# Linear-attention sums on one core: four heads and both signs of phi as one weight, 65 columns instead of 129, two PSUM banks instead of three, with due times and places annealed anew

## The chip, the cores and the metric

The program runs on one core of a Trainium2 chip. The metric is the time of one execution on the device in microseconds. Every time given here is the median of several executions, and the mean granted TensorE clock was between 0.996 and 1.0 in all profiled runs quoted.

Engines are named as in the profile: PE is TensorE, PEld its weight loads, DVE is VectorE, ACT is ScalarE, POOL is GpSimd, SP is SyncE, which issues most of the DMA.

## The reference

Two identical layers, each an attention without softmax over tokens (part A) and a gated MLP (part B), over 2048 tokens of width 512. Only part A is touched. H is 32 heads of width 16.

```python
def _A_ref(x, wqkv, w_phi, wo):                      # x is layer-normed
    q, k, v = ...                                    # [B, H, S, 16] each, from x @ wqkv
    pq = jnp.einsum("bhsd,hdf->bhsf", q, w_phi)
    pk = jnp.einsum("bhsd,hdf->bhsf", k, w_phi)
    phi_q = concatenate([softmax(pq), softmax(-pq)]) # 32 features: both signs of phi
    phi_k = concatenate([softmax(pk), softmax(-pk)])
    kv = jnp.einsum("bhsf,bhsd->bhfd", phi_k, v)     # the sums over all tokens
    z  = jnp.einsum("bhsf->bhf", phi_k)              # and the sum of phi itself
    num = jnp.einsum("bhqf,bhfd->bhqd", phi_q, kv)
    den = jnp.einsum("bhqf,bhf->bhq", phi_q, z)[..., None] + 1e-6
    return (num / den) ... @ wo
# x = x + A(norm(x)); x = x + MLP(norm(x)); twice
```

What matters: `kv` and `z` must be complete over all 16 token tiles (of 128 tokens) before any attention of that layer can start.

## The kernel before

The program is a list of operations, each with an engine, an estimated cost, a due time and the buffers that it takes and uses. When the program is built, a planner puts them in order: at each step it takes, of the operations that could start first, the one with the lowest due time. The order on each engine is then fixed; on the chip, engines only wait for each other's results and for buffers. The due times and a string of places (ACT or DVE for a copy, POOL or DVE for a phi) come from annealing on the planner's own costs.

```python
P, D, H, DH, NB, T, HB = 128, 512, 32, 16, 4, 16, 8
GV = P + 1                                           # 128 columns of v and one column of ones
p_q, p_b = psum("q", 3), psum("b", 5)                # 8 PSUM banks in all
p_ek, p_phi = pool("ek", 4, [2, D]), pool("phiK", 4, [2, D])
p_v = pool("vext", 5, [NB, GV])
# ... cut

class Keys:
    def __init__(self, l, before):
        self.bufs = [Buf(p_q) for _ in range(3)]     # held from the first token tile to R's build
    def tile(self, t, ...):
        # K = x Wk (PE), ek = exp(+-K) (ACT), V = x Wv (PE), vext <- V (ACT or DVE)
        # sk = sums of ek per head and sign (DVE, 128x64 <- 128x1024), 1/sk by ln and exp (ACT)
        # phiK = ek * 1/sk, two halves, each on DVE or POOL
        def kvz():
            for g in range(2 * NB):
                b, s = g // 2, g % 2                 # b: 8 heads, s: sign
                nc.tensor.matmul(self.bufs[g // 3].t[:, (g % 3) * GV:(g % 3 + 1) * GV],
                                 lhsT=ph.t[:, s, b * P:(b + 1) * P], rhs=vx.t[:, b, :],
                                 start=(self.n == 0 and g % 3 == 0), stop=(self.n == T - 1),
                                 skip_group_check=True)
    def build(self, due):                            # R: the sums, masked to each head's own block
        for k in range(3):
            ng = 3 if k < 2 else 2
            # num: R[:, 3k:3k+ng, 0:DH, :] = sums * Mf      128 x (ng*128)
            # den: R[:, 3k:3k+ng, DH, :]   = (z + eps/2) * Mf
# attend(): per token tile three groups of matmuls of R with Eq into PSUM buffers of p_q,
# copied out as N (numerators) and DS (denominators) by ACT or DVE
```

One weight holds eight heads of one sign; its product with `v` of those eight heads is 128x128, of which the mask keeps the eight 16x16 blocks on the diagonal.

The softmax here doesn't subtract the row's maximum and nothing guards it: scores larger than these inputs give would overflow.

Of the kernel before, what the change touches and what calls it, by code (L numbers as in the profile page):

```python
# [8 lines left out]
P = 128  # L9
D = 512  # L10
H = 32
DH = 16
# [7 lines left out]
GV = P + 1  # L20
# [183 lines left out]
DVE0 = (85, 170)  # L204
STATS = (592, 692)
# [11 lines left out]
class K:  # L217
# [9 lines left out]
    "0000010000001001000100000001010000000000101100111000110100010000100001001000000000100100101011010000"  # L227
    "1000000000111101000110100111010010111011010100100110101011010000101011001110000110000000111000000101"
    "1100101010101000101000110000000100000100110010110011011101000010011110010100010111101011111011011010"
# [9 lines left out]
    7238437, 6462738, 6444986, 6386567, 5992333, 6335033, 6406961, 6303369, 5712831, 6413612, 6092682, 6414331,  # L239
    7434675, 6620170, 4674366, 7071562, 5773774, 7071571, 7071548, 7071565, 5376048, 6430379, 5994524, 5038937,  # L240
    5154841, 6509440, 6825368, 6847621, 6377520, 5995707, 6404704, 6443663, 6844264, 5995988, 6959386, 6784947,
    6825065, 6420713, 6382495, 5410283, 6400005, 6216969, 7068818, 6425562, 6371338, 6325356, 5116853, 6509939,
    6325403, 6399345, 6420906, 6420903, 6403761, 5854885, 5527927, 6112383, 6040357, 6246638, 6429204, 6120059,
    6425464, 5996011, 5410344, 5937857, 5997209, 6629949, 6159020, 5837281, 6159017, 5812166, 6376057, 6112054,
    5527770, 5778741, 5859984, 6246016, 5780700, 6191478, 5995462, 6415371, 6420993, 5937862, 6218721, 6366108,
    6398876, 6355933, 6040362, 6353076, 6692318, 6246832, 6301941, 6333817, 6305472, 6420324, 6246635, 6282608,
    6010072, 6010132, 5937718, 5517502, 5527720, 5962872, 6417645, 6375834, 6115594, 6417622, 6376951, 6040201,
    6418805, 6367897, 6418065, 6246853, 6246635, 6280551, 6416172, 6413450, 5812833, 5734989, 5527730, 6415701,
    6589688, 6660152, 6259055, 6293340, 6418857, 6193613, 6400771, 6242577, 5594853, 5897821, 6418101, 6246214,
    6414310, 6418410, 6417781, 6293326, 6418213, 6337803, 6493628, 5823924, 6281803, 6385607, 6385616, 6414319,  # L250
    6392870, 6399165, 6376822, 6423098, 6382355, 6246148, 6189671, 6413294, 5970487, 6354744, 6354741, 6148511,
    6557117, 6415725, 7222162, 6412246, 6420372, 6418246, 6414304, 6330448, 6400107, 6407313, 6121354, 6246632,
    6247421, 6281496, 6418264, 6416104, 6292977, 6417603, 6446115, 6428567, 5823973, 6417942, 6323224, 6435617,
    6413175, 6372016, 6395620, 6424638, 6323105, 6245911, 6245802, 6350052, 6399800, 6339292, 6104846, 6199296,
    6400901, 6500288, 6429150, 6504253, 6415373, 5944333, 5942659, 6414885, 6419661, 6437686, 6424884, 6421739,
    6390896, 7006151, 6419612, 6444868, 6419927, 6419499, 6248090, 6668478, 6424284, 4761373, 6406555, 6435614,
    6323108, 6413172, 6425996, 6391320, 6135302, 6402710, 6374285, 6246461, 6335990, 6412253, 5985101, 5911850,
    6386514, 6397260, 6453191, 6347268, 6424767, 6407286, 6143060, 6143057, 6407535, 6396443, 6128422, 6067112,
    6334982, 7007584, 6247418, 6262299, 6338418, 6339077, 5945577, 5945498, 6399500, 6358459, 6363359, 6335893,
    6334988, 6334985, 6399098, 6149279, 9046332, 6270119, 6128455, 6017799, 5751499, 5578303, 6241820, 6237909,  # L260
    6228313, 6409033, 6434152, 6430501, 4770010, 6328230, 6191571, 6416107, 6349922, 7005684, 6415913, 6160440,
    6270116, 6017016, 6424993, 6190885, 6436945, 6398264, 6385936, 6409019, 6398261, 6830494, 6320125, 6349843,
    6270116, 6301355, 6394746, 6838656, 6782627, 6275299, 6301053, 6290656, 6025116, 5578252, 6382357, 6396063,
    6432980, 6476817, 6211202, 6228770, 6039495, 6004981, 6301064, 6161212, 6348404, 6160934, 6138010, 6350845,
    6275296, 5796164, 6025266, 6407917, 6382458, 6396463, 6502608, 6067109, 6415534, 4853830, 6415237, 5973986,
    6161241, 6353578, 6191119, 6350842, 6702118, 6992600, 6838653, 6366565, 6702501, 6264078, 6413974, 6362908,
    6362904, 6413355, 4467245, 6428734, 6412410, 6795872, 6752777, 6749932, 5860936, 5410347, 6354370, 6416428,
    6376372, 6441207, 6382099, 6417945, 6095059, 5543843, 5639763, 5236921, 6702312, 6802433, 6193610, 6293063,
    6418233, 6412932, 6417391, 6417541, 6412910, 5973743, 6432169, 6353603, 6418389, 6417785, 6418212, 6432986,
    6404484, 6419790, 6403799, 6504104, 6413197, 6402581, 6430185, 6421941, 6427775, 6317437, 6405598, 6149276,  # L270
    6067109, 6421649, 6426875, 6424701, 6424305, 6424600, 6431997, 6419066, 6427616, 6151465, 6421964, 6428658,
    6427976, 6422709, 6152793, 6428425, 6417633, 6429195, 6318384, 6422133, 6429703, 6429560, 6364528, 6798754,
    5236191, 6414580, 6296106, 6296113, 6054709, 5898871, 6296074, 5892919, 5617487, 5397065, 5397082, 3706746,
    5397079, 6419465, 5126265, 5416638, 3706278, 6415767, 6422610, 5124110, 6416965, 6625553, 5123800, 6416602,
    6419816, 6420908, 5396532, 5396822, 5497114, 7088606, 5592093, 5592116, 8111730, 6424461, 6419795, 6461520,
    6418906, 6421398, 6625766, 6420136, 6413037, 6424609, 6419798, 6425587, 5125608, 4328837, 3879494, 5115836,
    5126573, 6460663, 5847129, 6363148, 6422584, 5092781, 6419709, 5924498, 6237696, 6420096, 6427244, 6401061,
    6420862, 6421285, 6206071, 6156101, 6156036, 5302232, 5547741, 6373591, 6421404, 6060028, 6419415, 6048257,
    6419829, 5124239, 5126428, 6420346, 6431104, 6414424, 6420420, 6301789, 6982400, 5678438, 6154618, 6458766,
    6154597, 6156591, 6458649, 6427548, 6633825, 6444562, 6420766, 6006011, 6507274, 6421320, 6253412, 5547942,  # L280
    6421596, 6431444, 6336831, 6017869, 6957435, 6881846, 6972027, 6421334, 6350314, 6426586, 6250179, 6349612,
    6420979, 6409085, 6420596, 6419900, 6431585, 6431582, 6421968, 6430875, 6335448, 6348116, 6156140, 6448961,
    6426886, 6426258, 6434836, 6426677, 6425021, 6423370, 6420949, 5962145, 6205350, 6420178, 6420997, 6507473,
    6421435, 6337297, 5302335, 6253340, 6409377, 6446621, 6483667, 6272602, 6426074, 6429263, 6350262, 6426486,
    6421195, 6426208, 6448726, 6422715, 6336723, 6422336, 6423095, 6426531, 6349600, 6426322, 6453653, 6424950,
    6449358, 6416002, 6423415, 6411076, 6419851, 6422066, 6423162, 6425195, 6425012, 6424458, 6425647, 6425793,
    6423997, 6422141, 6425481, 6428769, 6424841, 6423823, 6423627, 6429536, 6425171, 6427675, 6426450, 6428704,
    6421366, 6431460, 6430235, 6423699, 6427448, 6423529, 6424778, 6431481, 6423189, 6279797, 6279298, 6418638,
    6421996, 6516407, 6517705, 6519047, 6426870, 6424741, 6423138, 6423148, 6422363, 6422859, 6424168, 6417327,
    6425272, 6425495, 6425628, 6424234, 6422881, 6424086, 6426119, 6424179, 6422682, 6424910, 6418638, 6426823,  # L290
    6425100, 6433715, 6430613, 6425871, 6428635, 6428822, 6424500, 6428773, 6427578, 6426097, 6424080, 6425359,
    6428061, 6424746, 6430015, 6420709, 6395980, 6491720, 6421893, 6336657, 6337082, 6422630, 6426207, 6426179,
    6424375, 6421663, 6425660, 6425930, 6422794, 6422276, 6425132, 6335341, 6425761, 6404996, 6383616, 6385581,
    6426169, 6427999, 6425677, 6426328, 6428760, 6428757, 6424969, 6428920, 6424083, 6424141, 6428548, 6424537,
    6428822, 6428197, 6427995, 6421391, 6428775, 6432602, 6425470, 6426425, 6424396, 6426336, 6426162, 6425753,
    6426483, 6430576, 6428349, 6429772, 6429237, 6429182, 6430031, 6402283, 6432374, 6426676, 6430764, 6435892,
    2595536, 5127000, 3705691, 6419739, 6236173, 3879702, 5846911, 6434442, 6421288, 6156356, 6312974, 6424365,
# [674 lines left out]
```

## Time and profile before

| | before |
|---|---|
| median time | 390.2 us (389.81 to 390.4, three executions) |
| span of the profiled execution | 388.6 us |
| PE busy, DVE busy | 379.0 us, 309.5 us |
| sums: matmuls, columns, start to start | 256, 129, 57 ns |
| last sum of layer one, first MLP matmul | 55.06 us, 67.38 us |
| first attention matmul of layer two | 243.29 us |

These are lines of the profile's page for the kernel before: the span, the busy time of PE with its share and count, and the chain of work that ended last, by engine.

```profile
span 388.6 us, 7611 instructions
PE 379.0 (98%) x2789; PEld 231.2 (60%) x2833; DVE 309.5 (80%) x785; ACT 217.7 (56%) x569; POOL 43.5 (11%) x45
PE 82%; DVE 7%; ACT 4%; DMA 3%; SPq 2%; issue 2%; DVEq 0%; ACTq 0%
```

PE is named for 82% of the chain. The 98% say less: the end of a matmul in this profile is modelled, and neighbours overlap. The Trainium skill ("Perfetto Trace Analysis", section Identifying the Most-Contended Engine) says that the busy share of matmuls is no good measure of the distance to the limit. So I used starts. In this trace a 512-column matmul is followed after 216 ns, one of 256 columns after 109, of 128 after 56, of 144 after 62. Where a start comes later than that, PE waited. In tables below, *PE waiting* is the sum over neighbouring matmuls of the start-to-start time minus columns/2.4 + 2.5 ns, with gaps left out that are longer by just one matmul's pace (those are records that the trace lacks). At the very start this reading fails: up to 4.7 us in this trace, starts come at half the pace (427 ns at 512 columns, 107 at 128), so waiting is counted from 13 us on. How the start goes differs from run to run: the first `sk` reduction on DVE starts at 11.9 to 12.6 us in the twelve traces of the new order. A time read from a single trace carries some tenths of a us for that reason.

Busy times by stretch, for the kernel before. The columns are the stretch, its length, and busy us (with the count of instructions) of PE, PEld, DVE, ACT and POOL, then PE's clock and the DMA.

```profile
13.00:57.00 44.00, 43.33 (x296) 23.86 (x300) 41.24 (x72) 40.75 (x120) 20.76 (x20) 1.00 0.73 169
57.00:80.00 23.00, 21.43 (x263) 16.59 (x262) 20.90 (x66) 18.52 (x55) 0.00 (x0) 1.00 0.11 22
180.00:250.00 70.00, 69.58 (x494) 43.56 (x500) 49.86 (x90) 48.81 (x121) 13.39 (x12) 1.00 0.09 18
```

From 13 to 57 us layer one's keys and sums are made, and DVE and ACT are nearly as full as PE. From 57 to 80 us attention starts. From 180 to 250 us layer two's sums are finished beside layer one's MLP, and DVE has 20 us free.

A burst of the sums in the timeline of the kernel before (start, length, engine, line, operation; x8 is eight instructions):

```profile
40.61 0.62 PE L678 MATMUL q<-vext,phiK 128*128 128x129 bf16 x8
...
41.07 0.38 PE L647 MATMUL b<-wv,xnTA 128*128 128x512 bf16 x1
```

Eight sums start at 40.61 and the next group starts at 41.07, 0.46 us later: 57 ns each. All 256 take 256 x 57 ns = 14.6 us of PE.

R's build in layer one of the kernel before, on DVE:

```profile
55.20 0.27 DVE L702 SCALAR_TENSOR_TENSOR R<-q,Mf 128x24 bf16<-128x24 f32 x2 [1.13 <-PE q L678]
55.39 1.34 DVE L695 TENSOR_TENSOR R<-q,Mf 128x384 bf16<-128x384 f32 x3
56.65 0.16 DVE L702 SCALAR_TENSOR_TENSOR R<-q,Mf 128x16 bf16<-128x16 f32 x1
```

It runs from 55.20 to 56.81 us, 1.6 us, and no attention can start before it ends.

### The profile page before, as it was taken

What the parts mean: (1) busy time and instruction counts of PE and PEld (TensorE: products, weight loads), DVE (VectorE), ACT (ScalarE), POOL (GpSimd) and SP (SyncE); (2) the same over time, 40 slices, a digit from 0 to 9 for tenths busy, and PEclk for the clock granted to TensorE, in tenths of its full rate; (3) what the DMA queues carried; (4) which work ended last, traced back from release to release, by engine and by line L of the source; (5) the groups of instructions that cost most, each with busy time, mean ns of one, the idle gap of its engine ahead of it and who ended that gap; (6) DMA issues with size and microseconds to landing.
All of it is one profiled execution on the core that took longest, in us unless ns stands there. A gap on an engine that the chain in (4) does not pass through costs nothing.

```text
span 388.6 us, 7611 instructions
## 1 busy us (share of the span) xinstructions
PE 379.0 (98%) x2789; PEld 231.2 (60%) x2833; DVE 309.5 (80%) x785; ACT 217.7 (56%) x569; POOL 43.5 (11%) x45
## 2 busy tenths in 40 slices
PE   8999998999999999999999999999999999999996
PEld 4555565957654554454667655578765545547674
DVE  6999979989999985479767486799997999455243
ACT  6999979744556545134665668976525520443111
POOL 0344620000200400012220122000000000000000
PEclk9999999999999999999999999999999999999999
DMA  8389730122322221102200000022233122201110
GB/s 245 105 187 189 209 102 1 37 55 50 79 57 42 56 53 29 27 16 54 43 0 15 14 15 0 2 33 62 57 71 81 38 51 65 54 7 29 56 35 29
DMA packets 60870, 22.84 MB, mean 59 GB/s; under 512 B 52672, under 2 KB 59808, under 8 KB 60832
## 3 DMA queue, kind: packets, MB, share of 16 engines
q1 hardware_dynamic: 60416, 21.95, 25.6%
q8 instruction: 22, 0.36, 0.4%
q10 hardware_dynamic: 416, 0.39, 0.3%
q14 instruction: 16, 0.13, 0.1%
HBM read 7.91 MB, written 2.10 MB: 26 GB/s over the span
## 4 chain that ended last, share of the span: by engine, by line
PE 82%; DVE 7%; ACT 4%; DMA 3%; SPq 2%; issue 2%; DVEq 0%; ACTq 0%
PE b L829 32%; PE b L862 19%; PE b L765 7%; PE b L641 5%; PE b L647 5%; PE b L715 4%; PE q L678 3%; PE b L805 3%; PE q L733 3%; ACT Eq L719 2%; DMA xnTA<-xn 1%; SPq L486 1%; DMA oT<-o 1%; ACT ek L644 1%; DVE N L564 1%
## 5 line engine op out<-in xcount | busy, mean ns | idle before, releaser
L829 PE MATMUL b<-xnTB,wgu 128*128 128x128 bf16 (+2 forms) x1192 | 149.9, 279 | 0.5
L829 PEld LDWEIGHTS <-wgu 128*128 128x128 bf16 x1200 | 97.8, 98 | 42.7
L862 PE MATMUL b<-wd,hT 128*128 128x512 bf16 (+2 forms) x348 | 82.1, 372 | 0.8
L833 ACT ACTIVATE gu<-b 128x512 bf16<-128x512 f32 (+1 forms) x83 | 48.1, 582 | 48.1 <-PE b L829 45.0
L661 POOL TENSOR_TENSOR phiK<-ek,sk 128x512 bf16<-128x512 bf16 x39 | 42.8, 1114 | 193.4 <-ACT sk L657 145.3
L862 PEld LDWEIGHTS <-hT 128*128 128x128 bf16 (+1 forms) x363 | 34.8, 98 | 34.9 <-DVE hT L837 0.3
L837 DVE TENSOR_TENSOR hT<-gu 128x512 bf16<-128x512 bf16 (+1 forms) x83 | 33.7, 407 | 18.6 <-ACT gu L563 17.0
L644 ACT ACTIVATE ek<-b 128x512 bf16<-128x512 f32 x64 | 36.0, 600 | 16.7 <-PE b L641 16.5
L652 DVE TENSOR_REDUCE sk<-ek 128x64 f32<-128x1024 bf16 x32 | 38.6, 1209 | 8.1 <-ACT ek L644 8.0
L563 ACT CAST gu<-b 128x512 bf16<-128x512 f32 (+1 forms) x46 | 26.1, 566 | 31.7 <-PE b L829 31.4
L719 ACT ACTIVATE Eq<-b 128x512 bf16<-128x512 f32 x64 | 35.4, 623 | 4.7 <-PE b L715 4.5
L564 DVE CAST gu<-b 128x512 bf16<-128x512 f32 (+1 forms) x37 | 25.0, 677 | 13.2 <-PE b L829 13.0
L869 DVE SCALAR_TENSOR_TENSOR X<-b,rsB,X 128x512 bf16<-128x512 f32 (+1 forms) x33 | 23.4, 725 | 15.1 <-PE b L862 15.0
L641 PE MATMUL b<-Wk,xnTA 128*128 128x512 bf16 x125 | 32.5, 379 | 0.4 <-DMA xnTA<-xn 0.3
L765 PE MATMUL b<-wo,oT 128*128 128x512 bf16 x121 | 31.7, 379 | 1.2 <-DMA oT<-o 0.8
L563 ACT CAST N<-q 128x384 bf16<-128x384 f32 (+1 forms) x63 | 27.9, 461 | 8.4 <-DVE pr L758 3.2
L647 PE MATMUL b<-wv,xnTA 128*128 128x512 bf16 x121 | 31.7, 379 | 0.4
L715 PE MATMUL b<-xnTA,Wq 128*128 128x512 bf16 x125 | 30.7, 379 | 0.2
L733 PE MATMUL q<-R,Eq 128*128 128x144 bf16 x256 | 26.8, 226 | 1.1 <-ACT N L563 0.5
L733 PEld LDWEIGHTS <-Eq 128*128 128x128 bf16 x256 | 19.9, 98 | 11.3 <-issue 1.4
L769 DVE TENSOR_TENSOR X<-X,b 128x512 bf16<-128x512 bf16 x32 | 21.5, 676 | 2.3 <-PE b L765 2.2
L610 DVE BATCH_NORM_STATS2 bstA<-X 128x6 f32<-128x512 bf16 x32 | 21.2, 681 | 1.8 <-DMA X<-in_A_x_dram 1.6
(71 smaller groups left out, 396.6 us busy)
## 6 DMA issues: line engine op xcount, KB each, us to landing
out_dram<-X SPq DMA_DIRECT2D x15, 128.0 KB, 1.7
X<-in_A_x_dram SPq DMA_DIRECT2D x6, 256.0 KB, 3.4
wgu<-in_B_W_gate_dram SPq DMA_DIRECT2D x4, 344.0 KB, 3.8
wgu<-in_B_W_up_dram SPq DMA_DIRECT2D x4, 344.0 KB, 4.6
wd<-in_B_W_down_dram SPq DMA_DIRECT2D x5, 256.0 KB, 4.5
wv<-in_A_wqkv_dram SPq DMA_DIRECT2D x2, 256.0 KB, 4.2
wo<-in_A_wo_dram SPq DMA_DIRECT2D x4, 128.0 KB, 3.1
oT<-o SPq DMA_TRANSPOSE x28, 2.4
```

Source lines behind the costliest of these rows:

```text
L563: both = {"ACT": ("ACT", act(cols), lambda: nc.scalar.copy(out=out_(), in_=in_()), False), "DVE": ("DVE", dve(cols), lambda: nc.vector.ten ...
L641: k = op("PE", mm(4, 512), due, lambda: [nc.tensor.matmul(kp.t[:], lhsT=xnTA[c][:, b, cols], rhs=Wk2[:, b, :], start=(b == 0), stop=(b == ...
L644: e = [op("ACT", act(512), due, lambda s=s: nc.scalar.activation(out=ek.t[:, s, :], in_=kp.t[:], func=AF.Exp, scale=1.0 - 2.0 * s), [k], [ ...
L647: v = op("PE", mm(4, 512), due_v, lambda: [nc.tensor.matmul(vp.t[:], lhsT=xnTA[c][:, b, cols], rhs=wv[:, b, :], start=(b == 0), stop=(b == ...
L661: e.tensor_tensor(out=ph.t[:].rearrange("p s (h f) -> p (s h) f", f=DH)[:, lo:lo + n], in0=ek.t[:].rearrange("p s (h f) -> p (s h) f", f=D ...
L715: q = op("PE", mm(4, 512), due(c, b), lambda b=b, qp=qp: [nc.tensor.matmul(qp.t[:], lhsT=Wq2[:, m, b * P:(b + 1) * P], rhs=xnTA[c][:, m, : ...
L719: done.append(op("ACT", act(512), due(c, b), lambda b=b, s=s, qp=qp: nc.scalar.activation(out=Eq[c][:, b, s, :], in_=qp.t[:], func=AF.Exp, ...
L733: pe.append(op("PE", mm(len(groups), GE), due, lambda ps=ps, groups=groups: [nc.tensor.matmul(ps.t[:, n * GE:(n + 1) * GE], lhsT=Eq[c][:, ...
L765: a = op("PE", mm(4, 512), due + 3, lambda: [nc.tensor.matmul(yp.t[:], lhsT=oT.t[:, b, :], rhs=wo[:, b, :], start=(b == 0), stop=(b == NB ...
L829: nc.tensor.matmul(ps.t[:, q * W:(q + 1) * W], lhsT=wgu[:, s, b, g * P:(g + 1) * P], rhs=xT.t[:, b, 0:W], start=(b == 0), stop=(b == NB - 1))
L833: nc.scalar.activation(out=gu.t[:, 0, 0:cols], in_=gp.t[:, 0:cols], func=AF.Relu)
L862: nc.tensor.matmul(yp.t[:, 0:c1 - c0], lhsT=h.t[:m, f * W + i * P:f * W + (i + 1) * P], rhs=wd[:m, f, c0:c1], start=(f == 0), stop=(f == N ...
```

## The change

One weight now holds four heads with both signs (4 x 2 x 16 = 128 columns), so its moving operand is only those four heads' 64 columns of v and the ones: 65 columns instead of 129. There are still eight matmuls and eight weight loads per token tile. The eight results fit two banks (4 x 65 = 260 columns each), so that `q` gives one bank to `b`. The layout of ek and phi follows. R's build takes four quarters of 64 partitions, since a sign is now half of the partitions, and R must be zeroed once. DUE and PLACE are new throughout.

```diff
+NG = 2 * NB
+HG = HB // 2
+GQ = P // 2
-GV = P + 1
+GV = GQ + 1
+SUMS = (8 * 40, 8 * 40 + 170)
-    p_q, p_b = psum("q", 3), psum("b", 5)
+    p_q, p_b = psum("q", 2), psum("b", 6)
-    p_ek, p_phi = pool("ek", 4, [2, D]), pool("phiK", 4, [2, D])
+    p_ek, p_phi = pool("ek", 4, [NG, 2, GQ]), pool("phiK", 4, [NG, 2, GQ])
-    p_v = pool("vext", 5, [NB, GV])
+    p_v = pool("vext", 5, [NG, GV + 1])
+    c_r0 = op("DVE", dve(1152, 4), 15000, lambda: nc.vector.memset(R[:], 0.0), ...)
-            self.bufs = [Buf(p_q) for _ in range(3)]
+            self.bufs = [Buf(p_q) for _ in range(2)]
-                for g in range(2 * NB):
-                    b, s = g // 2, g % 2
-                    nc.tensor.matmul(self.bufs[g // 3].t[:, (g % 3) * GV:(g % 3 + 1) * GV],
-                                     lhsT=ph.t[:, s, b * P:(b + 1) * P], rhs=vx.t[:, b, :],
+                for g in range(NG):
+                    b, k = g // 2, g % 2
+                    nc.tensor.matmul(self.bufs[k].t[:, b * GV:(b + 1) * GV],
+                                     lhsT=ph.t[:, g, :, :].rearrange("p s e -> p (s e)"), rhs=vx.t[:, g, 0:GV],
-            for k in range(3):                     # three num of up to 128x384, three den
+            for k in range(2):
+                for s in range(2):                 # four num of 64x256, four den
+                    rows, to = slice(s * GQ, (s + 1) * GQ), slice(k * GQ, (k + 1) * GQ)
+                    ...
# cut: the same access patterns in ek, sk, phi and vext; all of DUE (2112 numbers before, 2117 after)
# and most of PLACE (301 characters)
```

## The prediction

> **What bounds the kernel now.** TensorE, nearly everywhere. The page gives PE 379.0 of 388.6 us busy, but its ends are modelled, so I read starts. In the trace 512-column matmuls follow each other every 216 ns, 256 columns every 109, 128 every 56, 144 every 62: the rate at which columns stream ("TensorE: Matmul & The Clock Gate" of the Trainium skill, section on the back-to-back gap, has N/2.4 + 2.5 ns; the trace agrees). Against that rate, leaving out doubled gaps that are missing records, the stream loses only about 8 us: 1.3 before the first matmul, some 2.5 more to 10 us, 3.3 between 60 and 80 us, 3.4 after the last matmul. The granted clock is 1.0. DVE and ACT come near their limit only early: windows of 10 us from 10 to 50 us have DVE 9.0 to 10.0 and ACT 9.3 to 10.0 busy; 50 to 60 has slack. From 180 to 250 us, where layer two's sums are made, DVE has 50 of 70 us.
>
> **What the change removes.** The sums phi-transposed times v: 8 matmuls of 129 columns per token tile, 256 in all. In the timeline a burst of 8 starts at 40.61 and the next group at 41.07 us: 57 ns each, 14.5 us in all (the chain gives this line 3.1%). Now the moving part is 65 columns; weight loads stay at 256 of 128x128. The streaming rate would give 30 ns, but each matmul needs its own weight load: in the trace the next load starts 2 ns after a matmul's start, and where the engine had been waiting, the matmul followed its load by 31 ns (transposes at 10.73 us). So 33 ns at least; I estimate 36, range 30 to 45. Saving: 256 x (57 - 36) = 5.3 us (range 3 to 7).
>
> **What it adds.** A memset of R (about 0.4 us DVE, early). Building R: four products of 64 partitions x 256 and four small ones, instead of three of up to 128x384 (548 ns) and three small. Before it took 55.20 to 56.81 us; my estimate after is 2.1, so +0.5 us per layer, mostly covered by queries' matmuls.
>
> **What it moves.** Attention's three products per tile now share two PSUM banks. The timeline at 62 to 66 us shows PE already waiting for copies N and DS (0.42 and 0.49 us); this may grow by tenths. The rest gets six banks, which helps early. Due times and places are annealed again: I give that +-1.5 us.
>
> **How much counts.** Layer two's half of the sums lies in a dense matmul stream with slack on DVE and ACT: its 2.6 us should come through in full. Layer one's lies where DVE and ACT are also full, so part turns into waiting before 80 us: I count 1.4 us. Sum about 4 us: 390.2 to 386.2 us. Range 382.8 to 389.4. Faster by over 2% (under 382.4): 0.08; within 2%: 0.91; slower: 0.01.
>
> **What would show it.** Sums' matmuls starting every 30 to 45 ns instead of 57; PE busy down by some 5 us; layer two's attention starting (first matmul with R after 240 us) 3 us earlier or more; more PE waiting on ACT or DVE before 80 us, not after; R's build about 2 us.
>
> **What would make it wrong.** If the pair of load and matmul can't go below 50 ns, the gain is 1.5 us. If two banks make attention's matmuls wait at 57 to 80 and 240 to 255 us, the gain is lost. If six banks and the new order also remove the waiting between 60 and 80 us, the gain is 7 or 8 us.

## The result, and the profile after

The kernel after takes 388.21 us (387.5 to 388.71, six executions) beside 390.49 us (six executions) of the kernel before. The ratio is 0.9942, 95% interval 0.9928 to 0.9957: a gain of 0.58%, or 2.3 us. A ratio here is the mean time of one kernel's fast runs over that of the other's fast runs of the same rounds, so it is not quite the ratio of the medians.

| | before | after |
|---|---|---|
| median time beside each other | 390.49 us | 388.21 us |
| span of the profiled execution | 388.6 us | 386.3 us |
| PE busy, DVE busy | 379.0, 309.5 us | 374.1, 315.3 us |
| sums: start to start (median) | 57 ns | 32 ns |
| PE waiting 13 to 57 us | 0.9 us | 3.4 us |
| PE waiting 57 to 80 us | 3.0 us | 3.7 us |
| last sum of layer one, first MLP matmul | 55.06, 67.38 us | 55.33, 68.28 us |
| first attention matmul of layer two | 243.29 us | 240.37 us |

The same lines of the page, kernel after:

```profile
span 386.3 us, 7626 instructions
PE 374.1 (97%) x2787; PEld 225.2 (58%) x2831; DVE 315.3 (82%) x799; ACT 212.0 (55%) x559; POOL 45.3 (12%) x46
PE 76%; DVE 9%; ACT 3%; issue 2%; DMA 2%; POOL 0%; DVEq 0%; ACTq 0%
```

PE has 4.9 us less to do by this count, yet the time fell by only 2.3. Its share of the chain fell and DVE's rose. The stretches of the kernel after:

```profile
13.00:57.00 44.00, 41.62 (x297) 20.82 (x302) 43.20 (x72) 41.27 (x123) 20.75 (x19) 1.00 0.69 169
57.00:80.00 23.00, 20.86 (x222) 14.72 (x222) 22.05 (x77) 16.61 (x49) 0.00 (x0) 1.00 0.13 22
180.00:250.00 70.00, 68.96 (x520) 42.50 (x527) 52.50 (x104) 48.37 (x126) 15.54 (x13) 1.00 0.07 14
```

In the first stretch DVE's busy time rose from 41.24 to 43.20 of 44 us although it ran the same number of instructions there, 72, and PE's fell. The last sum of layer one started 0.3 us *later* than before, in spite of shorter sums (0.3 us is about what the start of a trace varies by; that it is not earlier is what counts). At the first attention matmul of layer two the kernel is 2.9 us ahead: all of the gain was made between 68 and 240 us, and 0.7 us of it was lost again after that.

A burst of the sums in the timeline of the kernel after, and the next group:

```profile
52.95 0.42 PE L719 MATMUL q<-vext,phiK 128*128 128x65 bf16 x8
...
53.20 0.59 PE L760 MATMUL b<-xnTA,Wq 128*128 128x512 bf16 x2
```

Eight sums in 0.25 us, 31 ns each. The shortening itself came as large as it could: 256 x (57 - 32) ns = 6.4 us of PE, more than the 5.3 predicted. R's build in layer one, kernel after:

```profile
55.56 0.43 DVE L741 TENSOR_TENSOR R<-q,Mf 64x256 bf16<-64x256 f32 x1 [0.40 <-PE q L719]
...
57.78 0.16 DVE L747 SCALAR_TENSOR_TENSOR R<-q,Mf 64x16 bf16<-64x16 f32 x1
```

It runs from 55.56 to 57.94 us, 2.4 us, 0.8 longer than before (predicted 0.5).

Layer one's half of the saving is 3.2 us, and yet the first MLP matmul comes 0.9 us later: about 4 us went somewhere before 68 us. Three candidates: DVE sets the pace there so that PE's saving is worth nothing (my theory, in part from the prediction); the longer build of R; two banks for attention. A fourth came from the trace and is shown with its experiments: the new order lets DVE run into POOL.

### The profile page after: what moved, and what is told of

It is laid out like the page before. It is cut to its first block, busy times and chain, and to the rows that moved or that the text cites. A ratio compares the mean times of both kernels' runs of the same rounds, so it can differ in the third digit from the quotient of the medians.

```text
span 386.3 us, 7626 instructions
## 1 busy us (share of the span) xinstructions
PE 374.1 (97%) x2787; PEld 225.2 (58%) x2831; DVE 315.3 (82%) x799; ACT 212.0 (55%) x559; POOL 45.3 (12%) x46
## 4 chain that ended last, share of the span: by engine, by line
PE 76%; DVE 9%; ACT 3%; issue 2%; DMA 2%; POOL 0%; DVEq 0%; ACTq 0%
PE b L874 34%; PE b L907 19%; PE b L810 6%; PE b L682 4%; PE b L688 4%; PE q L778 3%; PE b L850 2%; ACT Eq L764 2%; PE b L760 2%; DVE sk L693 2%; PE q L719 1%; DVE phiK L702 1%; DMA oT<-o 1%; DVE bstA L651 1%; DMA xnTA<-xn 1%
## 5 line engine op out<-in xcount | busy, mean ns | idle before, releaser
L702 POOL TENSOR_TENSOR phiK<-ek,sk 128x512 bf16<-128x512 bf16 x40 | 44.6, 1133 | 191.3 <-ACT sk L698 106.1
L605 DVE CAST gu<-b 128x512 bf16<-128x512 f32 (+1 forms) x42 | 28.0, 669 | 15.7 <-PE b L874 15.7
L604 ACT CAST gu<-b 128x512 bf16<-128x512 f32 (+1 forms) x41 | 23.2, 565 | 22.8 <-PE b L874 21.8
L778 PE MATMUL q<-R,Eq 128*128 128x144 bf16 x256 | 27.8, 226 | 1.4 <-ACT DS L604 0.8
L604 ACT CAST N<-q 128x384 bf16<-128x384 f32 (+1 forms) x60 | 26.7, 466 | 4.1 <-DVE pr L803 2.9
L855 ACT ACTIVATE gr<-b 128x192 bf16<-128x192 f32 (+1 forms) x19 | 5.8, 308 | 31.8 <-PE b L850 31.8
```

The costliest lines, as they stand in the source:

```text
L604: both = {"ACT": ("ACT", act(cols), lambda: nc.scalar.copy(out=out_(), in_=in_()), False), "DVE": ("DVE", dve(cols), lambda: nc.vector.ten ...
L702: e.tensor_tensor(out=ph.t[:].rearrange("p g s (h f) -> p (g s h) f", f=DH)[:, lo:lo + n], in0=ek.t[:].rearrange("p g s (h f) -> p (g s h) ...
L778: pe.append(op("PE", mm(len(groups), GE), due, lambda ps=ps, groups=groups: [nc.tensor.matmul(ps.t[:, n * GE:(n + 1) * GE], lhsT=Eq[c][:, ...
```

## The experiments

Twelve kernels were run, all with five rounds, each beside the kernel before. To compare two kernels of different rounds I compare their ratios to the kernel before; one hundredth of a ratio is 3.9 us. The difference of two such ratios is uncertain by about 0.0023, or 0.9 us, where each has an interval of +-0.0015 to 0.0018. The rounds ran on three chips (0, 1 and 7), and the kernel after was not run again in the later ones; `a_rbuild_half` (0.9938) and `a_spare` (0.9935), which turned out as fast as it, stand in for it there. All keep the order of existing instructions on every engine of the kernel that they start from, except where an edit says otherwise. A version of the new code with the old due times and two banks could not be built at all (the planner stops with "no instruction can go"; no run stands behind this), so that split of the change is not among the experiments.

### What the shortening is worth, layer by layer

`a_wide_both`, `a_wide_first` and `a_wide_second` are the kernel after with the sums widened again to 128 columns, in both layers or in one. Seven of every eight stream 63 columns too many, into PSUM columns that nobody reads; the result is right. (The ones fill one column more, so that there is something to stream.)

```diff
-  nc.tensor.matmul(self.bufs[k].t[:, b * GV:(b + 1) * GV],
+  nc.tensor.matmul(self.bufs[k].t[:, b * self.w:b * self.w + (self.w if g < NG - 1 else GV)],
-                   ... rhs=vx.t[:, g, 0:GV],
+                   ... rhs=vx.t[:].rearrange("p g e -> p (g e)")[:, g * (GV + 1):][:, 0:self.w if g < NG - 1 else GV],
+  self.w = P if l in LAYERS else GV      # R's build reads the groups at this step
```

> The kernel after, same instruction order on every engine, but 7 of every 8 sums' matmuls stream 128 columns again (the extra columns go to PSUM columns that nobody reads; result right). TensorE gets 224 x (56 - 33) = 5.2 us more work. If the shortening is worth its full size in this order, this takes 388.2 + 5.2 = 393.4 us, slower than the kernel before, so that the new order and the two banks would have cost about 3 us. If the early half is worth nothing because DVE and ACT set the pace there (my theory), about 388.2 + 2.6 = 390.8. If both halves were lost, 388.2.

> The kernel after with the sums of layer one alone widened to 128 columns (112 matmuls, 2.6 us of TensorE). My theory (DVE and ACT set the pace before 60 us): within 0.7 us of the kernel after, 388.2 to 388.9. The rival (order and banks are what cost, the shortening is worth its size in both layers): 390.8.

> The kernel after with the sums of layer two alone widened to 128 columns (112 matmuls, 2.6 us of TensorE). Both theories: about 390.8, as the matmul stream there has no gaps in either profile. If it comes out at 388.2, the slack is somewhere in layer two (the start of its attention at 248 us).

`b_narrow_both` goes the other way: the kernel before in its own order, but the sums of token tiles 2 to 16 stream only 65 of the 129 columns. Its output is wrong, which doesn't matter for the time.

```diff
-  b, s = g // 2, g % 2
-  nc.tensor.matmul(self.bufs[g // 3].t[:, (g % 3) * GV:(g % 3 + 1) * GV], ... rhs=vx.t[:, b, :],
+  b, s, w = g // 2, g % 2, P // 2 + 1 if self.n and self.l in (0, 1) else GV
+  nc.tensor.matmul(self.bufs[g // 3].t[:, (g % 3) * GV:(g % 3) * GV + w], ... rhs=vx.t[:, b, 0:w],
```

> The kernel before in its own instruction order, three banks and old build of R, but with the sums' matmuls of token tiles 2 to 16 cut from 129 to 65 columns (wrong result on purpose, 240 matmuls, 240 x (57 - 33) = 5.8 us of TensorE less). If the shortening is worth its size, 390.5 - 5.8 = 384.7, and the change lost 3.5 us in R's build, banks or order. My theory (early half worth nothing): 390.5 - 2.9 = 387.6.

Measured (median, then ratio to the kernel before; the last three columns are from starts in the traces):

| | time | ratio (95%) | PE waiting 13-57 us | last sum, layer one | first MLP matmul |
|---|---|---|---|---|---|
| before | 390.87 | 1 | 0.9 | 55.06 | 67.38 |
| after (its own rounds) | 388.21 | 0.9942 (0.9928 to 0.9957) | 3.4 | 55.33 | 68.28 |
| a_wide_first | 388.50 | 0.9943 (0.9925 to 0.9961) | 0.8 | 55.39 | 68.34 |
| a_wide_second | 390.80 | 1.0004 (0.9986 to 1.0022) | 3.3 | 54.93 | 67.88 |
| a_wide_both | 391.18 | 1.0010 (0.9994 to 1.0027) | 0.9 | 55.58 | 68.53 |
| b_narrow_both | 386.91 | 0.9901 (0.9880 to 0.9921) | 2.9 | 53.79 | 66.09 |

Widening layer two costs 1.0004 - 0.9942, 0.6% or 2.4 us. That is its full size within the noise (112 x 24 ns = 2.7 us). Widening layer one costs nothing that can be seen (0.0 us against the kernel after, 0.2 us for a_wide_both against a_wide_second, each +-0.9): the 2.5 us of PE waiting before 57 us simply turn into matmuls, and the last sum starts at the same time. In the order of the kernel after, the shortening of layer one is worth nothing, within this noise.

The first stretch of a_wide_first, in the same columns as above:

```profile
13.00:57.00 44.00, 43.08 (x296) 23.23 (x301) 42.17 (x72) 41.38 (x122) 21.00 (x19) 1.00 0.67 169
```

PE is as full as in the kernel before; DVE is still busy nearly all the time.

b_narrow_both is the surprise. In the *old* order, with three banks and the old build, the same shortening brings 1%, 3.9 us, almost exactly the 4 us that I had predicted for the change; there the last sum of layer one moves forward by 1.3 us. So in the old order the shortening is worth about 4 us, and the rest of the change gave back 1.6 us (+-1.0), before the first MLP matmul: 68.28 us instead of 66.09.

### Does DVE set the pace before 57 us?

`a_half_reduce` is the kernel after with the 16 reductions of layer one reading half of their elements; `a_half_reduce_wide` adds the widening of layer one.

```diff
-  in_=ek.t[:].rearrange("p g s (h f) -> p (g s h) f", f=DH), axis=AX.X
+  in_=ek.t[:].rearrange("p g s (h f) -> p (g s h) f", f=DH)[:, :, 0:DH // 2 if self.l == 0 else DH], axis=AX.X
```

> The kernel after in its own order, with the 16 reductions of layer one reading half of their elements (wrong result on purpose): DVE has about 9 us less to do before 55 us. If DVE sets the pace there, TensorE's waits before 57 us (3.4 us) go, the last sum ends by 53 us, and the time falls by 2 to 4 us, to 384.2 to 386.2. If ACT, DMA or TensorE set it: 387.7 to 388.2.

> As the one before, with the sums of layer one widened to 128 columns as well (2.6 us more for TensorE). With DVE relieved, TensorE should be what counts in the early stretch: my theory is 1.3 to 2.6 us more than the one before (while the same widening cost 0.2 us without the relief). If it again costs nothing, something other than DVE hides it.

Measured: a_half_reduce 385.88 us, ratio 0.9869 (0.9857 to 0.9882); a_half_reduce_wide 387.86 us, ratio 0.9920 (0.9907 to 0.9933). The comparison with the reference passed although the arithmetic is wrong: the wrong factor stands in both numerator and denominator of the attention and nearly cancels (an argument, not tested). The versions are not usable.

With DVE relieved, the first stretch of a_half_reduce reads:

```profile
13.00:57.00 44.00, 44.00 (x323) 22.55 (x322) 38.46 (x81) 43.75 (x128) 20.96 (x19) 1.00 0.66 170
```

PE is busy throughout (waiting 0.4 us instead of 3.4), with 26 matmuls more in the same stretch, and the last sum of layer one starts at 52.09 us instead of 55.33. The time falls by 0.9942 - 0.9869, 2.8 us. And the widening that cost nothing now costs 0.9920 - 0.9869, 2.0 us. This shows that DVE sets the pace there, and that it is what hides PE's saving. It is DVE's work that was relieved here, not the collisions described below: this trace still has 3.0 us of them. ACT (43.75 of 44 us) is then at its limit too.

### R's build and the two banks

`a_rbuild_half` stubs half of R's build, the numerators of one sign (wrong result), order unchanged. `a_spare` keeps the kernel after and its order, and puts every third group of attention's products, where one of the six `b` banks is unused over that part of the order, into that bank: 37 of the 256 matmuls in its trace, 16 of them between 57 and 80 us.

```diff
 # a_rbuild_half
-  out=R[to, s::2, 0:DH, heads], in0=...
+  out=R[to, s::2, 0:1 if s else DH, heads], in0=...[:, :, 0:1 if s else DH]
 # a_spare, after the order is made
+  for o in order:
+      if o.name == "erq":                    # attention's products
+          third += 1
+          free = [slots of p_b that no buffer holds from 12 places before o to 3 after its last user]
+          if third % 3 == 0 and free:
+              o.takes[0].pool, o.takes[0].slot = p_b, free[0]
```

> The kernel after in its own order, with half of R's build cut to a stub (wrong result on purpose): R's build falls from 2.4 to about 1.6 us in each layer, as before the change. If the longer build costs, up to 1.5 us less (386.7); my theory: it is on the way to attention in layer one, 0.4 to 0.8 us, 387.4 to 387.8; if covered by queries, 388.2.

> The kernel after in its own order, but about every third of attention's products (R with Eq) goes to one of the six other banks that happens to be free, so that attention has a third bank again where the profile of after shows waits (TensorE loses 3.7 us between 57 and 80 us, 0.95 of it in one wait at 60.5 us). If two banks cost the missing time, this gains 1 to 2 us, 386.3 to 387.3; my theory now: they cost little, at most 0.6 us, 387.6 to 388.3. It stays right.

Measured: a_rbuild_half 388.35 us, ratio 0.9938 (0.9922 to 0.9954); a_spare 388.38 us, ratio 0.9935 (0.9913 to 0.9957). Both agree with the kernel after (0.9942). R's build shrank less than I had expected, from 2.4 to 1.9 us (55.06 to 56.92) and not to 1.6, so this run takes back 0.5 of the 0.8 us. The traces settle the rest: the first matmul of attention starts 2.65 us after the last sum in the kernel before (57.71 and 55.06) and 2.66 us after it in the kernel after (57.98 and 55.33). The longer build was covered. I had expected a small gain, 0.4 to 0.8 us; that was wrong, or too small to see.

PE's waiting between 57 and 80 us stayed at 3.7 us with the third bank. The longest wait there, first in the kernel after and then in a_spare:

```profile
61.53 0.28 PE L778 MATMUL q<-R,Eq 128*128 128x144 bf16 x2 [0.78 <-ACT DS L604]
```

```profile
61.84 0.35 PE L778 MATMUL q<-R,Eq 128*128 128x144 bf16 x3 [1.15 <-ACT N L604]
```

In both PE waits until ACT has copied a bank of `q` out, and ACT is busy with the seven Eq before that, until about 61 us. The third bank lets PE run two matmuls ahead, and then it waits longer for ACT. So neither rival explains the loss in this order. An order made anew for three banks was not tried.

### What the new order does: DVE runs into POOL

Reading DVE's instructions one by one, the kernel after has four before 57 us that take longer than their like, each while a phi is running on POOL. Together they last 2.6 us longer than the usual time of the same instruction; in the kernel before the same count gives 0.3 us. Two of them are xn, the scaling of a normalized tile; the other two are phi at 44.04 and 49.48 us (1.02 and 1.54 us instead of 0.68). All sixteen xn of layer one (minimum, median and maximum in ns; first and last start in us), kernel before and then kernel after:

```profile
L621 DVE TENSOR_SCALAR xn<-X,mvA,rsA x16: 381/406/486, 5.0 to 43.5; 128x512 bf16<-128x512 bf16 x16
```

```profile
L662 DVE TENSOR_SCALAR xn<-X,mvA,rsA x16: 393/406/1121, 4.9 to 40.2; 128x512 bf16<-128x512 bf16 x16
```

The same median; but the longest is 1121 instead of 486 ns. DVE's timeline of the kernel after around those two:

```profile
16.87 0.68 DVE L651 BATCH_NORM_STATS2 bstA<-X 128x6 f32<-128x512 bf16 x1
17.47 1.09 DVE L662 TENSOR_SCALAR xn<-X,mvA,rsA 128x512 bf16<-128x512 bf16 x1
...
20.27 1.27 DVE L651 BATCH_NORM_STATS2 bstA<-X 128x6 f32<-128x512 bf16 x2
21.46 1.12 DVE L662 TENSOR_SCALAR xn<-X,mvA,rsA 128x512 bf16<-128x512 bf16 x1
```

POOL's timeline of the same kernel:

```profile
17.36 2.12 POOL L702 TENSOR_TENSOR phiK<-ek,sk 128x512 bf16<-128x512 bf16 x2 [0.17 <-ACT sk L698]
21.38 2.12 POOL L702 TENSOR_TENSOR phiK<-ek,sk 128x512 bf16<-128x512 bf16 x2 [1.91 <-ACT sk L698]
```

Each time POOL starts about 0.1 us before DVE, and DVE's xn ends 0.15 us after POOL's first phi (18.41 and 18.56, 22.44 and 22.59 us). The same holds for every long xn of this trace, the two of layer two included (0.15 us each); a long phi on DVE ends 0.54 or 0.55 us after POOL's. The Trainium skill describes this: in "SBUF — State Buffer", section SBUF: two separate sides, the port pair that DVE and GpSimd share is an exclusive lock, not a division of bandwidth; between a GpSimd instruction and one of DVE that uses that pair (by its mode, or for two SBUF inputs), whoever starts first has it for the whole instruction and the other waits. The trace agrees: 0.40 becomes 1.09 and 1.12 us, each ended by POOL's end. No record names the mode that xn ran in. In the planner's list the order is the other way round, xn from 16.85 and phi from 17.16 us; the planner knows of the port (these two times come from its list, not from a trace). But on the chip DVE was 0.62 us behind the list at that point and POOL only 0.19. This was the fourth candidate. It is a loss in exactly the stretch where DVE sets the pace.

`a_swap` moves three DVE instructions in the order, so that the xn at 17.5 and 21.5 us each come before a statistics instruction, and the second phi at 49.5 us comes after a reduction. `a_swap12` makes only the first two moves. `a_swap_spare` is a_swap with a_spare's third bank.

```diff
   order = arrange(ops)
+  late_of = {152: 138, 189: 156, 261: 329}      # a_swap12: without the last
+  for early, late in late_of.items():           # put the operation 'early' right behind 'late'
+      o = next(o for o in order if o.n == early)
+      order.remove(o)
+      order.insert(next(k for k, x in enumerate(order) if x.n == late) + 1, o)
```

> The kernel after with three places of DVE's order changed, nothing else: each time a statistics or phi instruction goes behind the one after it, so that DVE doesn't run into a phi on POOL (the profile of after has xn at 17.47 and 21.46 us take 1.09 and 1.12 us instead of 0.40, phi at 49.48 take 1.54 instead of 0.68). My theory (DVE sets the pace before 57 us, and these collisions are a loss that the new order brought): DVE gains 1.5 to 2 us, the last sum of layer one ends 1 to 2 us earlier than 55.3, and the time is 386.2 to 387.3 us. Rivals (two banks, or R's build, cost the missing time): 388.2, unchanged. It stays right.

> Only the first two of the three moves in DVE's order (the xn at 17.5 and 21.5 us), not the phi at 49.5 us. DVE should gain 1.1 to 1.4 us and may meet no collision at 49 us, because its lag on the plan is gone by then. 386.6 to 387.4 us. If the third move was the one that mattered: 388.0.

> The three moves in DVE's order and the third bank together, as a version that may beat both kernels: if the two are independent, the ratio of the three moves alone (0.9895) times what the third bank alone gains; 385.5 to 387.0 us. It stays right.

Measured: a_swap 386.91 us, ratio 0.9895 (0.9881 to 0.9909); a_swap12 386.68 us, ratio 0.9900 (0.9880 to 0.9919); a_swap_spare 387.30 us, ratio 0.9904 (0.9884 to 0.9923). All results are right. DVE's timeline of a_swap at the same place:

```profile
16.92 0.46 DVE L662 TENSOR_SCALAR xn<-X,mvA,rsA 128x512 bf16<-128x512 bf16 x1
17.30 0.68 DVE L651 BATCH_NORM_STATS2 bstA<-X 128x6 f32<-128x512 bf16 x1
...
20.41 0.40 DVE L662 TENSOR_SCALAR xn<-X,mvA,rsA 128x512 bf16<-128x512 bf16 x1
```

Both xn are short, and the last sum of layer one starts at 53.96 us (a_swap12: 53.65), 1.4 to 1.7 us earlier than in the kernel after (0.5 us of the 1.7 is a_swap12's earlier start: its first `sk` begins at 11.9 us, in the kernel after at 12.4). The time falls by 0.9942 - 0.9895, 1.8 us. The first two moves give all of it, as far as the noise lets one see. In a_swap12 the collision at 49 us still happens, against what I had expected of it (phi takes 1546 ns at 47.80 us); in a_swap it is gone but PE then waits 1.0 us for that phi. The third bank adds nothing again.

These moves leave a doubt: they also put xn earlier in DVE's order, which could help by itself. The last run removes it. `a_pool_later` leaves every instruction of the kernel after in its place and only makes POOL late: two tiny multiplications, whose result nobody uses, in front of the two phi that start at 17.36 and 21.38 us.

```diff
 # abridged
+  scr = new("scr", [1], F32)
+  # before the two phi on POOL:
+  for _ in range(2):
+      nc.gpsimd.tensor_scalar(out=scr[:], in0=sk.t[:, 0:1], scalar1=1.0, scalar2=None, op0=Alu.mult)
```

> The kernel after with every existing instruction of every engine in its place, and only POOL made later: two tiny multiplications (one element per partition, result unused) in front of its phi at 17.36 and of that at 21.38 us, so that DVE's xn at 17.47 and 21.46 us come first and POOL waits instead. If the collisions themselves are what costs (not the place of xn in DVE's order, which the moves also changed), both xn take about 0.4 us again, DVE gains about 1.4 us, and the time is 386.6 to 387.3 us, as with the moves. If the moves helped by putting xn earlier, 388.2. If the tiny instructions are too short to reverse the order, the profile shows xn at 1.1 us still and the run tells nothing. It stays right.

Measured: 386.28 us (386.12 to 386.8), ratio 0.9874 (0.9858 to 0.9891), result right. POOL's timeline of a_pool_later shows the first two tiny instructions, and the pair of phi behind them starts at 18.03 us instead of 17.36:

```profile
17.49 0.58 POOL L983 TENSOR_SCALAR scr<-sk 128x1 f32<-128x1 f32 x2 [0.18 <-ACT sk L698]
18.03 2.06 POOL L702 TENSOR_TENSOR phiK<-ek,sk 128x512 bf16<-128x512 bf16 x2
```

And DVE's timeline of it has both xn at their usual time:

```profile
17.60 0.40 DVE L662 TENSOR_SCALAR xn<-X,mvA,rsA 128x512 bf16<-128x512 bf16 x1
...
20.90 0.39 DVE L662 TENSOR_SCALAR xn<-X,mvA,rsA 128x512 bf16<-128x512 bf16 x1
```

Adding work to POOL made the whole program 0.9942 - 0.9874, 2.7 us faster, because POOL's phi then came second. (At the second place xn starts at 20.90 us and even the tiny pair only at 21.05, so without the first collision the second would probably not have come.) PE waits 1.9 us instead of 3.4 before 57 us, and the last sum starts at 54.00 us. In the kernel after, PE had stood 1.2 us at 26 us for the transposed tile of the second of these xn:

```profile
26.14 1.04 PE L682 MATMUL b<-Wk,xnTA 128*128 128x512 bf16 x4 [1.17 <-DMA xnTA<-xn]
```

The DMA that turns this tile was issued at 22.61 us, right after the long xn, and landed at 26.09. In a_swap and in a_pool_later that wait is gone. (The transfer's own time is not the reason: 3.5 us in the kernel after and also in a_pool_later, 2.4 us in a_swap.) So the collisions themselves are what cost. a_pool_later is also the fastest correct version of all: 1.26% faster than the kernel before and 0.7% faster than the kernel after.

## Why the prediction was right or wrong

- **The time and the range: right.** 388.21 us lies in 382.8 to 389.4, and "within 2%" came true. The gain is 2.3 us where I had said 4. The range, 0.8 to 7.4 us of gain, was wide enough to hold the result with one of the two terms of the gain missing, so its being right says little for that term.
- **What bounds the kernel: right, with a limit.** From 80 us on PE waits only 1.4 us in the kernel before and 2.9 us in the kernel after. Before 57 us DVE is the one, more strictly than I had put it.
- **The cost of a load and matmul pair: right in kind, estimated too high.** I said 36 ns, range 30 to 45; the median is 32, and the shortest are 29, so the floor of 33 that I had derived does not hold. The saving of PE is 6.4 us rather than 5.3.
- **Layer two's half comes through in full (2.6 us): right.** Widening it again costs 2.4 us (+-0.9). Layer two's attention starts 2.9 us earlier; I had said 3 or more.
- **Layer one's half, "I count 1.4 us": this is the term that was mis-sized.** In the kernel after it is worth 0.0 us, +-0.9 (a_wide_first, 0.9943 beside 0.9942). In the old order the full shortening gave 3.9 us; less the 2.4 of layer two, about 1.5 is left, and in that trace the last sum of layer one comes 1.3 us earlier, so the term was good for the old order. What was wrong is that I held the new order to be as good as the old one. In the new order DVE loses 2.6 us to POOL before 57 us, and DVE sets the pace there. Removing two of these collisions returns 1.8 to 2.7 us, and the result, 386.3 to 386.9, is what I had predicted for the change.
- **"Annealed again: +-1.5 us": right as a caution, empty as a reason.** The loss, 1.6 us (+-1.0), lay in that term. The old profile does show such collisions, but only in layer two (two xn of 1.15 and 1.21 us instead of 0.41, at 180.15 and 188.44 us), where DVE has time to spare. That a new order would bring them into layer one could not be read from it.
- **R's build +0.5 us, mostly covered: right.** It grew by 0.8 us, and neither a_rbuild_half nor the start of attention after the last sum (2.65 and 2.66 us) shows a cost.
- **Two banks: the risk that I named did not come.** With a third bank for 37 of the matmuls, in the same order, PE's waiting at 57 to 80 us stays at 3.7 us. Six banks removed no waiting there either.
- **"More PE waiting before 80 us, not after": half right.** Between 13 and 80 us PE waits 3.2 us more (7.1 instead of 3.9), after it 1.5 us more (2.9 instead of 1.4).

What stays open: PE waits 3.2 to 3.7 us between 57 and 80 us in every version with the new order, and I did not find out how much of it could be had. The two later collisions of layer one (at 43 and 48 us there) and three of layer two remain in the fastest version. Why a_pool_later is 0.2 to 0.3% faster than the moves is not settled; their intervals overlap in part.

## What to carry to other kernels

Where a second engine sets the pace, work taken from the main engine can be worth nothing: widen it again in that stretch alone and see whether the time moves. A fixed order made on estimated costs can lose, to a resource that two engines lock such as the port of DVE and POOL, as much as the change gains; look for instructions much longer than their median and at what runs beside them. The cure can be to delay the engine that has time, here by two pieces of useless work of 0.6 us on POOL.

## What the Trainium skill lacked or had wrong

- "TensorE: Matmul & The Clock Gate", Back-to-back issue gap, gives for a stream of load and matmul pairs a sustained pace of about 81 ns at 128 columns and about 131 ns at 512. The pairs pace at 56 ns and 216 ns: they follow the formula that this section calls that of isolated matmuls, N/2.4 + 2.5 ns, and at 512 columns no two starts were less than 215 ns apart.
- The same page gives no pace for pairs below 128 columns in bf16. Here it is a median of 32 ns at 65 columns (29 to 35 for the middle eight of ten within bursts, the formula gives 30), with a full 128x128 load before each, so such a load costs at most a few ns beside 65 columns (in b_narrow_both the median is 29).
- "SBUF — State Buffer", SBUF: two separate sides, has the lock right. It gives no time for a pair of compute instructions like these: a 128x512 bf16 scaling on DVE took 1.09 and 1.12 us instead of 0.40 when a phi on POOL (1.06 us) had started 0.1 us before, and it ended 0.15 us after POOL's phi, sooner than its own 0.40 us after it.
- Beyond the advice in the same page's summary to schedule whichever of the two is off the critical path, no page says how to cure it by delaying GpSimd; two pairs of instructions of one element per partition, each pair about 0.6 us in the profile, gained 2.7 us here.
